# Second-half weights in quarters, own outputs in one bank, U rows by TensorE and integer sums on GpSimd, in the first steps of an mLSTM and feed-forward kernel

## The chip, the cores and the metric

The kernel runs on one core of one Trainium2 chip. The metric is the device time of one execution in microseconds (us). Three runs of the kernel before gave 424.73, 424.93 and 425.49, median 424.93.

## The reference, cut to what matters

Two blocks follow each other. The first is an mLSTM cell over 4 batches, 8 heads, 768 tokens and 40 numbers per head; the second is a multiplicative feed-forward block over the 3072 tokens.

```python
for t in range(S):                                  # per batch and head
    m_new = max(f[t] + m, i[t])
    C = exp(f[t] + m - m_new) * C + exp(i[t] - m_new) * outer(v[t], k[t])
    n = exp(f[t] + m - m_new) * n + exp(i[t] - m_new) * k[t]
    m = m_new
    y[t] = sigmoid(o[t]) * (C @ q[t]) / max(abs(n @ q[t]), 1)
x = y as (3072 tokens, 320)
out = ((x @ w1) * (x @ w2)) @ w3 @ w_out            # w1, w2: 320x1024; w3: 1024x1024; w_out: 1024x320
```

All four weights come as 64-bit floats, so 128 rows of 512 weights are 512 KB.

## The kernel before, in words

The cell is computed in 24 units `n`, each 128 tokens of one batch with all 8 heads; the tokens of a unit are two halves of 64. A unit has a table `pw` (rows of `U`, then `Exp` on ScalarE, then a mask on GpSimd), the scores `ss` (kT by qT), the state update `pc`, the **own output** `ph` (`pw` by `v`, within the halves) and the **output from the state** `pi`. VectorE multiplies `ss` into `pw` (line 402), updates the state (409 or 411, and 419) and makes the output `y` (lines 430 to 457).

The work is written out as steps `s = 0, 1, 2, ...` of the last loop (line 829). In step `s`, TensorE does, in the order of the code: the first part (`up`, 16 passes of 128x256) of the feed-forward products of that step, the transposes of k and q for a later unit (`turn`, where it stands), `up_rest` (the last 64 rows of x, weights `wr`), `ph` and `pi` of unit `s-1`, `ss` and `pc` of unit `s`, then the transposes `px` of a finished `y` (`x_trans`) and those of k and q (`turn`, tile `pt`) of unit `s+1`. `in_order` (line 84) makes the order of the code the order of TensorE; the other engines also run their instructions in the order in which they stand. Step 2 is written out apart, in `between` (line 902): there TensorE does the first `px` and the first `up`. `warm` (line 97) puts matmuls whose result nobody reads into the tile `fill`.

`up` takes two blocks `f` of 128 columns of w1 and w2 at a time: steps 2 and 3 use f = 0..3 (the first halves), step 4 uses f = 4, 5, step 5 uses f = 6, 7, and from step 6 on there are two `up` per step, over all columns.

Weights are fetched as raw 64-bit words (`fetch`, line 216, on the SP queue), scaled on ScalarE (`scale`, lines 196 and 200: the high and the low words), and put together on VectorE (`to_f32`: line 204 shifts, line 205 adds integers; the adder is GpSimd for `w_out` alone). `convert()` does this for the next tile in the list; `n_cvt[s]` says how many times at the end of step `s`. The raw words go into idle parts of later tiles (`idle`, line 529) and, when that list is empty, into four rotating buffers `raw`. The second halves of w1, w2 and `wr` are five tiles (512 columns each), fetched in step 2 between the loads of unit 4 and converted in `between`, at the end of step 2 and in step 3 (`late`). Then come 8 tiles of w_out and 16 of w3, which VectorE also transposes (line 253); step 8 converts three tiles of w3. `fold` (line 258) multiplies finished w3 tiles with w_out (tile `wp`) from step 10 on.

The rows of `U` for a unit are made on VectorE (`rows_of_u`, line 300, up to unit 9); unit 0 takes them by TensorE instead (`spread`, line 277: 16 matmuls of 96 rows by 64 columns into the tile `ub`). `N_DIAG = 2`: for units 0 and 1 `ph` has a PSUM tile of its own and one VectorE addition (line 434); for units 2 to 9 it is laid out in the quarters of `cell[1]` and takes four additions (line 440).

PSUM has 8 banks: two tiles `cell` of two banks each, and four banks that rotate (`mps`) over `px`, `pt`, `pa`, `pb`, `ub`, `ph`, `fill`, `wp`: a new tile waits for the last reader of the tile four allocations earlier.

Of the kernel before, what the change touches and what calls it, by code (L numbers as in the profile page):

```python
# [16 lines left out]
def kernel(  # L17
# [26 lines left out]
    nc = tc.nc  # L44

    B, H, S, D = q.shape
    L = 64
    P = 128
    NT = S // L
    NT2 = S // P  # L50
    NU = NT2 * B
# [39 lines left out]
    def mm(out, lhsT, rhs, start=True, stop=True):  # L91
        in_order(nc.tensor.matmul(out, lhsT=lhsT, rhs=rhs, start=start, stop=stop))  # L92
# [1 line left out]
    def transpose(out, in_, n=P):  # L94
        in_order(nc.tensor.transpose(out, in_, ident[0:n, 0:n]))  # L95

    def warm(n, m=4, small=0):
        bank = mps([P, 4, P], "fill")
        for _ in range(n):
            mm(bank[:, 0:m], ident, ident.unsqueeze(1).to_broadcast([P, m, P]))  # L100
        for i in range(small):
            r = halves[i % 2]
            mm(bank[r, 0, 0:L], ident[r, 0:L], ident[r, 0:L])

    halves = [slice(0, L), slice(L, P)]
    heads = [slice(0, D), slice(DP, DP + D)]
# [2 lines left out]

    NB, NBQ, NBV = 4, 3, 5  # L110
    N_DVE = N_U = 10
    N_DIAG, N_OWN = 2, 10
    q_all = const.tile([P, NBQ * H * DP], FP, name="q_all")
    qbuf = [q_all[:, i * H * DP:(i + 1) * H * DP].rearrange("p (h d) -> p h d", d=DP) for i in range(NBQ)]
    kbuf = [const.tile([P, H, DP], FP, name=f"kbuf{i}") for i in range(NB)]
# [86 lines left out]
    def to_f32(dst, raw, adder):  # L202
        bits = dst.bitcast(U32)
        nc.vector.tensor_scalar(out=bits, in0=raw[:, :, 1], scalar1=3, scalar2=None, op0=OP.logical_shift_left)
        adder.tensor_tensor(out=bits, in0=bits, in1=raw[:, :, 0], op=OP.add)  # L205

    def cols(c0, n):
        return slice(2 * c0, 2 * (c0 + n))
# [7 lines left out]
    def fetch(kind, i, part):  # L216

        if kind == "w12":
            c0 = part * CW
            if i < 2 * KF:  # L220
                wt, src = ((w1, w1_d), (w2, w2_d))[i // KF]
                ko = i % KF
                dst, pieces = wt[:, ko, c0:c0 + CW], [(every, src[ko * 128:(ko + 1) * 128, cols(c0, CW)])]
            else:
                dst, pieces = wr[:, c0:c0 + CW], [(slice(j * REM, (j + 1) * REM), src[KF * P:DM, cols(c0, CW)])
                                                  for j, src in enumerate((w1_d, w2_d))]
        elif kind == "wo":
            dst, pieces = wo[:, i, :], [(every, wo_d.rearrange("(p i) n -> p i n", i=FO)[:, i, :])]
        else:
            dst, pieces = None, [(square, w3_d[i * 128 + part * 64:i * 128 + (part + 1) * 64, cols(j * CQ, CQ)]  # L230
                                  .rearrange("(m r) n -> r m n", m=2)) for j, square in enumerate(squares)]
        pend.append((dst, raw_tile(dst.shape[-1] if dst is not None else CW, pieces), i, part))
# [9 lines left out]
    def convert():  # L242
        if not scaled:
            scale_next()
        dst, raw, ko, half = scaled.pop(0)
        if dst is not None:
            to_f32(dst, raw, nc.gpsimd if dst.shape[-1] == DM else nc.vector)
            return
        w3 = wst.tile([128, CW], FP, name="w3", tag="w3")
        to_f32(w3, raw, nc.vector)  # L250
        if half == 0:
            w3T_t[ko] = wst.tile([128, FO, 128], FP, name="w3T", tag="w3T")
        nc.vector.transpose(out=w3T_t[ko].rearrange("c k (m r) -> c m k r", r=32)[:, 2 * half:2 * half + 2],
                            in_=w3.rearrange("r (m c k) -> r m k c", m=2, k=FO))
        if half:
            turned_w3.append(ko)
# [20 lines left out]
    def spread(n):  # L277


        ub = mps([P, H, L], "ub")  # L280
        for h in range(H):
            r = n % B * H + h
            for x in range(2):
                mm(ub[halves[x], h, :], ident[0:RG, r:r + 1].to_broadcast([RG, L]), U[:, x * L:(x + 1) * L])
        return ub

    def cols_of_u():
# [14 lines left out]

    def weights(n):
        c, b = divmod(n, B)
        src = weights_tile(n) if n else spread(n)
        pw = weights_tile(n)
        for h in range(H):
            nc.scalar.activation(out=pw[:, h, :], in_=src[:, h, :], func=AF.Exp, bias=aT[:, c, b * H + h:b * H + h + 1])  # L308
# [34 lines left out]
    def quarter_work(s, rest, between, late):  # L343
# [10 lines left out]
        if 0 <= n < NU:  # L354
            pw, vt, qT = u_t.pop(n), vbuf[n % NBV], qT_t.pop(n)
            before = before_t.pop(n)
            if n < N_DIAG:
                warm(1)

            if n < N_DIAG:  # L360
                ph = mps([P, H, D1], "ph")
                for hq in range(H):
                    for r in halves:
                        mm(ph[r, hq, :], pw[r, hq, :], vt[r, hq, :])
            for hd in range(H // 2 if n >= N_DIAG else 0):
                for x, e in quarters:
                    hq = hd if x == e else hd + H // 2
                    mm(ph[x][halves[e], hd, :], pw[halves[x], hq, :], vt[halves[x], hq, :])
            for p in range(NP):
                for hip, x in quarters if n >= B else quarters[1:3]:  # L370
                    mm(pi[halves[x], hip, p, :], qT[heads[hip], p, halves[x]], before[x][heads[hip], p, :])
# [154 lines left out]
    load(1)  # L526
    fetch("w12", 2, 0)
    load_o(0)
    idle += [words[:, i * CW:(i + 1) * CW] for words in (w3o_words, wo_words) for i in range(2)]
    fetch("w12", 3, 0)  # L530
    load_o(1)
    fetch("w12", 4, 0)
# [285 lines left out]
    n_seven = [0] * 19 + [1] * 12 + [0]  # L818
    n_down = [0] * 16 + [2] * 5 + [1] * 4 + [0] * 7
    n_out = [0] * 27 + [1, 0, 1, 0, 3]  # L820
    w12 = [("w12", i, part) for part in range(2) for i in range(2 * KF + 1)]
    todo = w12[5:] + [("wo", i, 0) for i in range(FO)] + [("w3", ko, part) for ko in range(FO) for part in range(2)]
    n_cvt = [0, 0, 2, 0, 1, 2, 3, 3, 3] + [2] * 6
    n_fetch = [5, 5, 10]
    pinned, ahead = 32, 9
    behind = ExitStack()
# [2 lines left out]
    for s in range(len(n_up)):  # L829
# [3 lines left out]
            load_u(s + 3)  # L833
        if s < 3:
            if s == 2:
                for _ in range(3):
                    fetch(*todo.pop(0))
            load(s + 2, slice(0, 2))
            if s == 1:
                load_o(2)  # L840
            if s == 2:
                for _ in range(2):
                    fetch(*todo.pop(0))
                fetched = 10
            load(s + 2, slice(2, 3))
            if s:
                load_o(s + 2)
        elif s + 2 < NU:
            load(s + 2)
            load_o(s + 2)  # L850
        if s < NU:
            if s >= B:
                decayed(state[s % B][1], state[s % B][0], s, 0)
# [48 lines left out]
        def between():  # L902
            twice(1)
            weighted(2)
            rows_of_u(3)
            for _ in range(3):
                scale_next()
            for n in range(2):
                x_trans(n)
                if n == 0:  # L910
                    warm(1, small=38)
            for _ in range(3):
                convert()
            turn(2)
            block = up(*now[0])
            weighted(3)
            weights(3)
            masks(3)
            out_gate(2)
            convert()  # L920
            up_rest(*block)

        gated = None
# [4 lines left out]
        with tc.issue_after(gated.ins) if gated else nullcontext():  # L928
            if seven:
                seven[3]()  # L930
            for _ in range({NU: 1, NU + 1: 3}.get(s, 0)):
                next(wsums)
            if s == NU + 1:
                ab_sums(*summed.pop(0))
            if NY <= s - 2 < NU:
                x_turn(s - 2)
            for n in () if s == 1 else (s + 2,) if s < B else (s + 2, s + 3) if s == B else (s + 3,):
                if n < N_U:
                    rows_of_u(n)
            if N_DVE <= s + 1 < NU:  # L940
                shift(s + 1)
                gated = turn(s + 1)
            if s - 2 in range(4 * GT - 1, NU, GT):
                token_sums((s - 2) // GT)
            if s < len(n_up) - 2 and n_out[s + 1] and s > NU + 2:
                ab_sums(*summed.pop(0))
# [6 lines left out]
            cell_psum.close()  # L953
            banks.extend([ps_m] * 3 + [ctx.enter_context(tc.tile_pool(name="ps_x", bufs=4, space=bass.MemoryType.PSUM))] * 4)
        if s in (2, 3):
            turned, converted = 2, converted + (4 if s == 2 else 2)
        while turned < min(s - 1, NY):
            x_trans(turned)
            turned += 1
        if s + 1 < N_DVE and s not in (1, 2):  # L960
            turn(s + 1)
        if s < NU:
            if 0 < s < NU - 1 and s != 2:
                if s != 1:
                    weighted(s + 1)
                if s <= NY:
                    weights(s + 1)
                if 2 < s < N_DVE:
                    twice(s - 1)
                masks(s + 1)  # L970
            if s != 2 and s <= NY:
                out_gate(s)
# [4 lines left out]
            for i, r in enumerate(third):  # L977
                nc.sync.dma_start(out=U_d[i * GC:(i + 1) * GC].rearrange("c r t -> r c t"), in_=U3[r])
        with tc.issue_after(gated.ins) if N_DVE <= s + 1 < NU else nullcontext():
            for _ in range(n_cvt[s] if s < len(n_cvt) else 0):  # L980
                convert()
                converted += 1
        if s >= ahead:
# [40 lines left out]
```

## Time and profile before

| | |
|---|---|
| median of 3 runs | 424.93 us |
| the profiled execution | 425.0 us, span 423.3 us |
| granted TensorE clock | 1.00 |
| PE busy | 414.0 us (98%) |
| PEld busy | 335.9 us (79%) |
| DVE busy | 296.0 us (70%) |
| ACT busy | 183.0 us (43%) |
| POOL busy | 165.4 us (39%) |
| DMA | 46.56 MB, mean 110 GB/s |

PE is TensorE's matmuls, PEld its weight loads, DVE VectorE, ACT ScalarE, POOL GpSimd, SP the queue that issues most transfers. A timeline row has start, duration, engine, line, operation, tile written <- tiles read, shape, count, and in brackets the idle time before it and what ended it. An fp32 matmul appears as two passes, so 16 matmuls are a count of 32. All matmuls have line 92 and all PE transposes line 95 (helpers), so tile names tell them apart.

### The profile page before, as it was taken

The page shows a single profiled execution, that of the slowest core. Times are in us where ns is not written, and L with a number is a line of the kernel's source. Part 1 is how long each engine was busy: PE and PEld are TensorE (multiplying, and loading weights), DVE is VectorE, ACT ScalarE, POOL GpSimd, SP SyncE. Part 2 cuts the span into 40 slices and gives each one's busy share as a digit, 9 for nine tenths or more (in the row PEclk, how much of TensorE's full clock was granted, in tenths as well). Part 3 has the DMA queues.
Part 4 walks back from the last instruction along what each step waited for, and adds up shares of the span by engine and source line. Part 5 has one row for each costly group of instructions (what it writes and reads, how often), then busy time and mean ns, then how long its engine had stood idle before and what let it go on. Part 6 is the DMA issues. An engine that isn't in the chain of part 4 may idle for free.

```text
span 423.3 us, 13077 instructions
## 1 busy us (share of the span) xinstructions
PE 414.0 (98%) x5353; PEld 335.9 (79%) x5353; DVE 296.0 (70%) x561; ACT 183.0 (43%) x516; POOL 165.4 (39%) x219
## 2 busy tenths in 40 slices
PE   8999999999999999999999999999999999999997
PEld 4778788887787787888777778688778779888896
DVE  5676995688948768767635747396877598575972
ACT  3875775567734735843745334253422210210000
POOL 3441373443303303303457343457453487542100
PEclk9999999999999999999999999999999999999999
DMA  8998989689993584863417762733221110000001
GB/s 187 213 152 239 214 153 157 163 180 174 203 192 104 122 175 109 170 104 58 104 35 158 149 139 76 147 73 83 55 54 30 26 39 6 28 2 31 2 33 62
DMA packets 124555, 46.56 MB, mean 110 GB/s; under 512 B 104720, under 2 KB 116304, under 8 KB 124496
## 3 DMA queue, kind: packets, MB, share of 16 engines
q1 hardware_dynamic: 120896, 41.70, 49.2%
q10 hardware_dynamic: 3600, 4.03, 2.7%
q8 instruction: 42, 0.69, 0.7%
q14 instruction: 17, 0.14, 0.1%
HBM read 39.91 MB, written 5.80 MB: 108 GB/s over the span
## 4 chain that ended last, share of the span: by engine, by line
PE 84%; DVE 6%; DMA 3%; issue 2%; SPq 2%; ACT 1%; POOL 1%; DVEq 0%; POOLq 0%; ACTq 0%
PE cell L92 21%; PE pa L92 20%; PE pb L92 13%; PE wp L92 8%; PE o L92 8%; PE po L92 6%; PE p L92 3%; DMA raw<-in_moe_w_dram 2%; PE px L95 2%; PE pt L95 1%; DVE pw L779 1%; DMA q_all<-in_q_dram 1%; SPq L158 1%; DVE ab L693 1%; SPq L139 1%
## 5 line engine op out<-in xcount | busy, mean ns | idle before, releaser
L340 POOL TENSOR_TENSOR state<-state,decay 128x164 f32<-128x164 f32 x40 | 23.2, 581 | 139.7 <-DVE state L409 112.6
L92 PE MATMUL pa<-xT,w 128*128 128x256 f32 x240 | 60.4, 382 | 0.0
L92 PEld LDWEIGHTS pa<-xT,w 128*128 128x128 f32 x240 | 44.4, 190 | 6.4
L308 ACT ACTIVATE pw<-pw,aT 128x64 f32<-128x64 f32 x184 | 46.5, 339 | 0.8 <-DVE pw L300 0.5
L92 PE MATMUL pb<-xT,w 128*128 128x256 f32 x192 | 45.6, 380 | 0.2 <-DVE w L205 0.2
L738 POOL TENSOR_TENSOR ab<-ab,a_sb 128x512 f32<-128x512 f32 x22 | 29.4, 1359 | 31.7 <-DVE ab L693 31.7
L92 PEld LDWEIGHTS pb<-xT,w 128*128 128x128 f32 x192 | 36.4, 190 | 5.5 <-DVE w L205 0.6
L720 POOL TENSOR_TENSOR wo<-wo 128x512 f32<-128x512 f32 x22 | 27.5, 1269 | 29.0 <-DVE wo L695 29.0
L92 PE MATMUL pa<-xT,wr 64*64 64x256 f32 x384 | 37.0, 386 | 0.6 <-DVE wr L205 0.6
L92 PE MATMUL wp<-wo,w3T 128*128 128x320 f32 x128 | 35.9, 433 | 1.4 <-issue 0.8
L92 PE MATMUL pb<-xT,wr 64*64 64x256 f32 x384 | 36.4, 380 | 0.0
L313 POOL TENSOR_SCALAR_AFFINE_SELECT pw<-pw 64x512 f32<-64x512 f32 x48 | 33.2, 692 | 7.9 <-ACT pw L308 6.4
L647 ACT ACTIVATE a_sb<-pa 128x512 f32<-128x512 f32 x24 | 14.3, 597 | 49.9 <-PE pb L92 49.9
L648 DVE TENSOR_TENSOR ab<-pb,a_sb 128x512 f32<-128x512 f32 x24 | 16.4, 688 | 27.4 <-ACT a_sb L647 27.2
L92 PE MATMUL cell<-w3o,ab 128*128 128x320 f32 x128 | 35.5, 433 | 0.0
L92 PEld LDWEIGHTS wp<-wo,w3T 128*128 128x128 f32 x128 | 23.8, 190 | 10.9 <-issue 1.0
L92 PEld LDWEIGHTS cell<-w3o,ab 128*128 128x128 f32 x128 | 24.2, 190 | 9.6 <-ACT wo L711 0.2
L92 PEld LDWEIGHTS pa<-xT,wr 64*64 64x64 f32 x384 | 18.9, 132 | 15.5 <-issue 8.8
L695 DVE SCALAR_TENSOR_TENSOR a_sb<-pa,wo 128x512 f32<-128x512 f32 x12 | 8.3, 689 | 31.1 <-PE pa L92 31.1
L437 ACT COPY h<-cell 64x164 f32<-64x164 f32 x56 | 16.3, 290 | 31.5 <-DVE y L430 31.0
L92 PE MATMUL po<-w3o,ab 128*128 128x320 f32 x96 | 26.4, 433 | 0.0
L92 PEld LDWEIGHTS po<-w3o,ab 128*128 128x128 f32 x96 | 18.1, 190 | 7.3
(185 smaller groups left out, 883.0 us busy)
## 6 DMA issues: line engine op xcount, KB each, us to landing
raw<-in_moe_w_dram SPq DMA_DIRECT2D x64, 128.0 KB, 3.1
kbuf<-in_k_dram SPq DMA_DIRECT2D x24, 160.0 KB, 4.3
v_all<-in_v_dram SPq DMA_DIRECT2D x24, 160.0 KB, 4.7
o_in<-in_o_gate_dram SPq DMA_DIRECT2D x24, 160.0 KB, 4.8
pw<-U_d SPq DMA_DIRECT2D x28, 128.0 KB, 3.5
raw<-in_moe_w_dram SPq DMA_DIRECT2D x5, 512.0 KB, 6.3
raw<-in_moe_w_out_dram SPq DMA_DIRECT2D x8, 320.0 KB, 4.1
out_dram<-o_sb ACTq DMA_DIRECT2D x14, 160.0 KB, 2.4
```

The costliest lines, as they stand in the source:

```text
L92: in_order(nc.tensor.matmul(out, lhsT=lhsT, rhs=rhs, start=start, stop=stop))
L95: in_order(nc.tensor.transpose(out, in_, ident[0:n, 0:n]))
L139: nc.sync.dma_start(out=dst, in_=rows(src, n))
L308: nc.scalar.activation(out=pw[:, h, :], in_=src[:, h, :], func=AF.Exp, bias=aT[:, c, b * H + h:b * H + h + 1])
L313: nc.gpsimd.affine_select(out=pw[r], in_=pw[r], compare_op=OP.is_ge, fill=0.0, base=0, pattern=[[0, H], [1, L]], channel_multiplier=-1)
L340: nc.gpsimd.tensor_tensor(out=new, in0=old, op=OP.mult, in1=decay[:, b * NP:(b + 1) * NP, 2 * c + x:2 * c + x + 1] .to_broadcast([P, NP, D1]))
L437: nc.scalar.copy(out=h[halves[x], 0:H // 2] if x == e else h[halves[x], H // 2:H], in_=ph[x][halves[e]])
L647: nc.scalar.mul(out=a_sb, in_=pa, mul=UP ** -2)
L648: nc.vector.tensor_tensor(out=ab_t[gr][j][:, fs[0]:fs[-1] + 1, t0:t0 + a_sb.shape[-1]], in0=pb, in1=a_sb, op=OP.mult)
L695: nc.vector.scalar_tensor_tensor(out=out, in0=p, scalar=UP ** -2, in1=q, op0=OP.mult, op1=OP.add)
L720: aside_by.tensor_tensor(out=kept[j][:, 1:4:2], in0=kept[j][:, 1:3], in1=kept[j][:, 3:4].to_broadcast([128, 2, TH]), op=OP.add)
L738: aside_by.tensor_tensor(out=t[:, f:FO:FH, :], in0=t[:, f:FO:FH, :], in1=a, op=OP.mult)
```

## The change

Four things change in the first ten steps; the rest of the program is the same.

1. The second halves of w1, w2 and `wr` become two quarters (256 columns): ten tiles for five. The first five go into idle words of `wo` and are fetched in step 2 ahead of the loads of unit 4; the other five go into words of `w3o` and are fetched in step 3. `load_o` moves one step later from unit 3 on. Step 2 fetches 5 tiles of 256 KB in place of 5 of 512 KB.
2. The integer sum (line 205) of these ten tiles is done on GpSimd; the shift stays on VectorE. The five first quarters are converted at the end of step 2 and in step 3, the five last ones in step 4, ahead of `out_gate` and behind the copies of the transposes of unit 5. `n_cvt` becomes 3, 5, 2, 3, 3, 4 for steps 2, 4, 5, 6, 7, 8 (before: 2, 1, 2, 3, 3, 3): step 7 converts three tiles of w_out (before: two, and one of w3), and step 8 four tiles of w3 (before three).
3. `N_DIAG = 6`: the own outputs of units 2 to 5 also get a bank of their own and one addition.
4. The `U` rows of units 4 and 5 come from `spread` (their `Exp` reads `ub` from PSUM), no longer from `rows_of_u`.

In `between`, `rows_of_u(3)` moves behind three `convert()` (the fourth is dropped there), and `warm(1, small=38)` becomes `warm(2)`.

```diff
-    N_DIAG, N_OWN = 2, 10
+    N_DIAG, N_OWN, SPREAD = 6, 10, (0, 4, 5)
...
         if kind == "w12":
-            c0 = part * CW
+            c0, n = ((0, CW), (CW, CW // 2), (CW + CW // 2, CW // 2))[part]
...
-            to_f32(dst, raw, nc.gpsimd if dst.shape[-1] == DM else nc.vector)
+            to_f32(dst, raw, nc.vector if dst.shape[-1] == CW else nc.gpsimd)
...
-                mm(ub[halves[x], h, :], ident[0:RG, r:r + 1].to_broadcast([RG, L]), U[:, x * L:(x + 1) * L])
+                t0 = n // B * P + x * L
+                mm(ub[halves[x], h, :], ident[0:RG, r:r + 1].to_broadcast([RG, L]), U[:, t0:t0 + L])
...
-        src = weights_tile(n) if n else spread(n)
+        src = spread(n) if n in SPREAD else weights_tile(n)
...
-            if n < N_DIAG:
+            if n < 2:
                 warm(1)
...
-    idle += [words[:, i * CW:(i + 1) * CW] for words in (w3o_words, wo_words) for i in range(2)]
+    idle += [w3o_words[:, i * CW:(i + 1) * CW] for i in range(2)]
+    idle += [words[:, i * CW // 2:(i + 1) * CW // 2] for words, order in ((wo_words, range(5)), (w3o_words, (4, 0, 1, 2, 3)))
+             for i in order]
...
-    w12 = [("w12", i, part) for part in range(2) for i in range(2 * KF + 1)]
+    w12 = [("w12", i, part) for part in range(3) for i in range(2 * KF + 1)]
...
-    n_cvt = [0, 0, 2, 0, 1, 2, 3, 3, 3] + [2] * 6
+    n_cvt = [0, 0, 3, 0, 5, 2, 3, 3, 4] + [2] * 6
...
             if s == 2:
-                for _ in range(3):
+                for _ in range(5):
                     fetch(*todo.pop(0))
             load(s + 2, slice(0, 2))
             if s == 1:
                 load_o(2)
             if s == 2:
-                for _ in range(2):
-                    fetch(*todo.pop(0))
+                load_o(3)
                 fetched = 10
             load(s + 2, slice(2, 3))
-            if s:
-                load_o(s + 2)
         elif s + 2 < NU:
-            load(s + 2)
-            load_o(s + 2)
+            load(s + 2, slice(0, 2))
+            if s == 3:
+                for _ in range(5):
+                    fetch(*todo.pop(0))
+                fetched = 15
+            load(s + 2, slice(2, 3))
+            load_o(s + 1)
...
-            rows_of_u(3)
             for _ in range(3):
                 scale_next()
             for n in range(2):
                 x_trans(n)
                 if n == 0:
-                    warm(1, small=38)
+                    warm(2)
             for _ in range(3):
                 convert()
+            rows_of_u(3)
             turn(2)
...
             out_gate(2)
-            convert()
             up_rest(*block)
...
-                if n < N_U:
+                if n < N_U and n not in SPREAD and s != B:
                     rows_of_u(n)
...
         if s + 1 < N_DVE and s not in (1, 2):
             turn(s + 1)
+        if s == B:
+            for _ in range(n_cvt[s]):
+                convert()
+                converted += 1
+            for n in (6, 7):
+                rows_of_u(n)
```

More of the change, by code (lines that the diff above doesn't have):

```diff
@@ L95, in transpose, with warm @@
         in_order(nc.tensor.transpose(out, in_, ident[0:n, 0:n]))
-    def warm(n, m=4, small=0):
+    def warm(n, m=4):
         bank = mps([P, 4, P], "fill")
@@ L100, in warm @@
             mm(bank[:, 0:m], ident, ident.unsqueeze(1).to_broadcast([P, m, P]))
-        for i in range(small):
-            r = halves[i % 2]
-            mm(bank[r, 0, 0:L], ident[r, 0:L], ident[r, 0:L])
     halves = [slice(0, L), slice(L, P)]
@@ L222, in fetch @@
                 ko = i % KF
-                dst, pieces = wt[:, ko, c0:c0 + CW], [(every, src[ko * 128:(ko + 1) * 128, cols(c0, CW)])]
+                dst, pieces = wt[:, ko, c0:c0 + n], [(every, src[ko * 128:(ko + 1) * 128, cols(c0, n)])]
             else:
-                dst, pieces = wr[:, c0:c0 + CW], [(slice(j * REM, (j + 1) * REM), src[KF * P:DM, cols(c0, CW)])
+                dst, pieces = wr[:, c0:c0 + n], [(slice(j * REM, (j + 1) * REM), src[KF * P:DM, cols(c0, n)])
                                                   for j, src in enumerate((w1_d, w2_d))]
@@ L841 @@
             if s == 2:
-                for _ in range(2):
-                    fetch(*todo.pop(0))
+                load_o(3)
                 fetched = 10
             load(s + 2, slice(2, 3))
-            if s:
-                load_o(s + 2)
         elif s + 2 < NU:
-            load(s + 2)
-            load_o(s + 2)
+            load(s + 2, slice(0, 2))
[5 more added lines that the diff above has]
+            load_o(s + 1)
+        elif s + 2 == NU:
+            load_o(s + 1)
         if s < NU:
@@ L955 @@
         if s in (2, 3):
-            turned, converted = 2, converted + (4 if s == 2 else 2)
+            turned, converted = 2, converted + (3 if s == 2 else 2)
         while turned < min(s - 1, NY):
@@ L979 @@
         with tc.issue_after(gated.ins) if N_DVE <= s + 1 < NU else nullcontext():
-            for _ in range(n_cvt[s] if s < len(n_cvt) else 0):
+            for _ in range(n_cvt[s] if s < len(n_cvt) and s != B else 0):
                 convert()
```

## The prediction

> **What bounds the kernel now.** I read the page first: TensorE is busy nearly throughout, and the chain that ended last runs over it.
>
> ```profile
> PE 414.0 (98%) x5353; PEld 335.9 (79%) x5353; DVE 296.0 (70%) x561; ACT 183.0 (43%) x516; POOL 165.4 (39%) x219
> PE 84%; DVE 6%; DMA 3%; issue 2%; SPq 2%; ACT 1%; POOL 1%; DVEq 0%; POOLq 0%; ACTq 0%
> ```
>
> So only time that TensorE idles, or spends on passes of no use, can be won, and every useful pass that is added costs its full time, unless it falls into a wait. The windows by stage tell where it idles: 58 to 104 us has none at all, the changed stretch a little.
>
> ```profile
> 28.00:50.00 22.00, 20.90 (x407) 17.45 (x406) 15.32 (x33) 15.32 (x38) 5.47 (x9) 1.00 0.95 199
> 50.00:58.00 8.00, 8.00 (x177) 7.01 (x176) 7.49 (x20) 5.29 (x16) 4.95 (x9) 1.00 1.03 246
> 58.00:104.00 46.00, 46.00 (x751) 39.38 (x753) 35.02 (x72) 29.87 (x78) 21.21 (x33) 1.00 0.85 162
> 104.00:106.50 2.50, 1.87 (x77) 1.51 (x70) 2.47 (x5) 2.26 (x8) 0.00 (x0) 1.00 0.86 234
> ```
>
> Columns: stretch, length, then busy us (instructions) of PE, PEld, DVE, ACT, POOL; clock, DMA share, GB/s. Last, the timeline of the changed steps and of step 9: what TensorE waits for, and the rows that price the additions.
>
> ```profile
> 9.07 1.98 PE L92 MATMUL ub<-gates,ident 96*64 96x64 f32 x32
> 20.93 1.07 PE L92 MATMUL ph<-v_all,pw 64*64 64x41 f32 x30
> 21.78 0.25 PE L92 MATMUL cell<-state,qT 40*64 40x41 f32 x1
> 23.76 3.39 PE L92 MATMUL fill<-ident 128*128 128x512 f32 x78
> 25.29 0.24 POOL L486 COPY y<-y 128x64 f32<-128x64 f32 x1 [1.75 <-DVE y L457]
> 40.56 0.56 PEld L92 LDWEIGHTS cell<-qT,kT 40*64 40x64 f32 x32 [0.47 <-ACT qT L330]
> 44.94 1.16 PEld L92 LDWEIGHTS pb<-xT,w 128*128 128x128 f32 x6 [0.59 <-DVE w L205]
> 47.05 0.13 PEld L92 LDWEIGHTS pa<-xT,wr 64*64 64x64 f32 x1 [0.95 <-DVE wr L205]
> 57.78 0.89 POOL L205 TENSOR_TENSOR wo<-wo,raw 128x320 uint32<-128x320 uint32 x1
> 102.99 0.39 DVE L204 TENSOR_SCALAR w<-raw 128x512 uint32<-128x512 uint32 x1
> 103.52 0.69 DVE L205 CUSTOM_DVE_ANT_0 w<-raw,w 128x1024 uint16<-128x1024 uint16 x1
> 104.24 1.12 DVE L253 STREAM_TRANSPOSE w3T<-w 128x512 f32<-128x512 f32 x1
> 105.29 1.25 DVE L648 TENSOR_TENSOR ab<-pb,a_sb 128x512 f32<-128x512 f32 x2
> 105.99 8.88 PE L92 MATMUL wp<-wo,w3T 128*128 128x320 f32 x32 [0.63 <-DVE ab L648]
> ```
>
> The waits before the change are for qT (its copy stands on ScalarE behind the scaling of raw words) and for the converted second halves, w at 44.94 and `wr` at 47.05. At step 9 VectorE is the late one: three w3 conversions run without a gap into `ab`, and `wp` wants the bank that `ab` frees.
>
> **Step 2 to the px of step 5 (27.08 to 49.78 before).** Start to start, the groups take: px 0.38, pt pair 0.87, up 3.46 (two of 1.73 in the chain), up_rest 0.91 (54.59 to 55.50), ph, pi, ss, pc 1.82 (55.50 to 57.32). Step 2 without ph and pi is 6.54, steps 3 and 4 without px 7.06 each: 20.66 of work in 22.70, so 2.04 us of waiting.
> Won: the px of unit 1 starts at 27.08, behind 76 small passes, though its input was ready at 25.53 (POOL row). Two fills (4 passes of 0.43) end at 25.5, so px starts at 25.57: -1.5. The waiting for w and `wr` goes, since the first quarters are half the words, shifted in step 3, and five GpSimd sums of about 0.71 finish by about 43.5, ahead of pa and pb (about 43.4 and 45.1). The 0.71 is an estimate: a sum of 128x320 takes 0.89, one of 128x164 (line 340) 0.47, 256 columns lie between. The qT wait goes too, since three scalings of 256 columns fit ahead of the copies. Together -2.04.
> Paid: `ub` of unit 4 stands between pt and pa of step 4. Its price is from the same group at 9.07, 1.91 to what follows; bounds are 1.98 above and 0.85 below, the `ph` group, whose 32 passes run two side by side. I take 1.91, the same operation. [...]
> `ph` in a bank of its own runs on two quadrants, 0.85 (20.93 to 21.78) for 0.44 in `cell`: +0.41 each, for units 2 and 3 +0.82.
> A new wait: in step 3 the bank of `ph` is that of `pa`, four allocations back, so `ph` waits for `a_sb` (line 647), which starts 0.29 after up_rest and takes 0.60: +0.91, between 0 (if banks turn otherwise) and 0.91. In steps 4 and 5 the bank is that of a pt, long free; in step 6 that of the first of two `up`, read while the second rests: 0. Behind this wait stand pi, ss, pc and all of step 4.
> Sum: -1.5 -2.04 +1.91 +0.82 +0.91 = +0.1; px of step 5 at 49.9.
>
> **Step 5.** Before, it had no wait. Now it needs the last quarters, whose five scalings stand on ScalarE behind the qT copy of unit 5 (about 51.4; a pair each 0.69, by the 0.395 spacing of 320 columns and 0.555 of 512) and whose shifts stand on VectorE behind y of unit 3. That y ended 2.84 after the reciprocal at 51.94; now the additions are one of 0.50 for four of 1.34, the reciprocal comes at about 50.3 and y ends at 53.1. First shift 53.4, first sum 54.1, second 54.8, third 55.5, fourth 56.2, `wr` 56.9. TensorE is through pt at 51.1 and `ub` of unit 5 at 53.0; pa waits until 54.15, its second matmul until 54.85, then all is there: waiting 1.4. With `ub` 1.91 and `ph` 0.41 the step is 3.7 longer. If `ub` were shorter, the wait would grow by as much. Sums of 0.47 or 0.95 (bounds: the 164 columns and a little over the 320) make it 0.5 less or 0.6 more.
> What speaks against this move is in the rows: shifts of 320 columns took 0.66 beside a GpSimd mask (55.93), 512 columns without one 0.39. [...]
> VectorE's relief elsewhere (five sums of 0.69, four times 0.84 for the additions, two `rows_of_u` of 0.70) I cost at nothing: no TensorE wait from 50 to 104 hangs on it. The moved loads (o gates a step later, v and o behind the quarters on SP) I also cost at nothing: ScalarE has work ahead of each o gate, and steps 4 and 5 start no earlier than before.
>
> **Steps 6 and 9.** `ph` of unit 5: +0.41. Step 8 converts four w3 tiles for three. VectorE is gapless there, one tile is 2.29 (102.99 to 105.29), and `ab` stands behind it: `wp` starts 2.29 later. Step 7 is lighter by one, but has its slack in a wait of 0.25 for `a_sb`, and y of step 8 follows TensorE, not VectorE's queue. +2.29, between 0 and 2.9 (the first tile, beside GpSimd, took that).
>
> **Sum** against the profiled 425.0 (0.07 over the median, as good as equal): +0.1 +3.7 +0.4 +2.3 = +6.5, so 431.5. Low end: `ub` 0.9 in step 4 (-1.0), no wait for `a_sb` (-0.9), short sums (-0.5), and half of the 2.3 hidden, 428.0. High end: long sums (+0.6) and half or more of the late transfers below, 434.
>
> **Rivals.**
> Hidden conversion: VectorE makes up the fourth w3 tile and step 9 keeps its 0.63 wait. For it: step 8 comes after a lighter step 7. Against: no gap from 97.9 to 106.5. 431.5 - 2.3 = 429.2. Chance 0.13.
> Late quarters: the third quarter's scaling stands ahead of the kT and qT copies of unit 3 on ScalarE. The three 512 KB tiles were scaled at 33.81, 36.50 and 38.30, each after waiting for its transfer. Quarters at half their spacing are there by 35.2; from about 36.0 on the wait reaches TensorE, and if the third came at 38.3 as before, it would cost 2.3: 433.8. Chance 0.12.
> Faster: steps 2 to 6 are paced by the supply of weights, and the added passes run beside their neighbours, as the 32 `cell` passes of `ph` do in 0.44. Then 3.5 is won there and two groups of 0.43 are paid, the sums being ready: 422.3. It decides as soon as all added TensorE time, 5.5 in my rows, and the new waits stay under 3.5. For it: two of the three waits before are for weights. Against: the row at 9.07, and 50 to 104 us without a TensorE wait. Chance 0.07, and 0.02 that it ends within 0.2%.
> That the order is not what the text says is ruled out by the list of instructions: two `ub` groups ahead of pa, ten GpSimd sums, four w3 tiles in step 8.
>
> **How the numbers follow.** My forecast has 0.66, the rivals 0.13, 0.12 and 0.09. Two tenths of a per cent, 0.85 us, is about what a measurement of this kernel can tell from no change. Slower: 0.66 + 0.13 + 0.12 = 0.91; same 0.02; faster 0.07. The range 428.0 to 434.0 takes in the first three cases and the bounds of `ub`, the sums and the new wait.
>
> **What would show it.** Right: two `ub` groups near 41 to 53 us of about 1.9; `ph` of unit 2 waiting for `a_sb`; px of step 5 near 49.9; pa of step 5 waiting for a GpSimd sum of line 202 and starting near 54; px of step 6 near 61 (before 57.3); `wp` waiting about 2.9 for `ab`. Wrong: px of step 6 at or before 58, `ub` under 1 us, or `wp` with a wait of 0.6.

## The result and the profile after

The changed kernel takes 430.19 us (430.0 to 431.0), the kernel before, run beside it, 424.86 us: ratio 1.0126, 95% interval 1.0109 to 1.0144. The profiled execution took 430.02 us, span 428.3 us. Taken again later it was 430.81 against 425.34, ratio 1.0129 (1.0093 to 1.0165). Ratios leave out the runs in a slow state, such as those over 1.5% above the fastest of the same kernel; medians include them.

First the page of the changed kernel, engines and chain of waits, then its windows by stage (stretch, length, busy us of PE, PEld, DVE, ACT, POOL, clock, DMA share, GB/s).

```profile
PE 417.0 (97%) x5343; PEld 338.6 (79%) x5343; DVE 287.8 (67%) x547; ACT 183.3 (43%) x526; POOL 172.3 (40%) x229
PE 88%; DVE 5%; DMA 2%; issue 2%; POOL 1%; ACT 1%; SPq 0%; DVEq 0%; POOLq 0%
```

```profile
28.00:50.00 22.00, 21.50 (x462) 18.37 (x460) 11.79 (x30) 14.09 (x41) 10.39 (x16) 1.00 1.00 196
50.00:62.00 12.00, 8.97 (x160) 7.04 (x160) 5.07 (x11) 4.94 (x18) 7.45 (x11) 0.86 0.92 189
62.00:108.00 46.00, 46.00 (x655) 39.56 (x653) 26.80 (x59) 28.74 (x77) 20.89 (x32) 0.96 0.57 127
108.00:113.00 5.00, 5.00 (x169) 4.03 (x168) 4.52 (x8) 3.85 (x10) 0.00 (x0) 1.00 0.87 225
```

The loss is in the second row: TensorE, without a gap there before, idles 3.0 of 12 us, and the granted clock is 0.86. The stretch of steps 2 to 4 (first row) is better filled than before, and that of step 9 (last row) has lost its gap. Where the clock fell is seen by cutting the trace at the starts of its 3.41 us stretches:

```profile
48.94:52.35 3.41, 1.76 (x24) 1.20 (x21) 2.39 (x7) 3.41 (x12) 2.31 (x4) 1.00 0.92 128
52.35:55.76 3.41, 3.41 (x9) 2.71 (x9) 1.56 (x3) 2.00 (x10) 3.35 (x7) 0.50 0.92 304
59.18:62.59 3.41, 1.54 (x71) 1.37 (x64) 1.58 (x5) 0.00 (x0) 0.00 (x0) 1.00 0.47 62
62.59:66.00 3.41, 3.41 (x14) 3.04 (x13) 2.70 (x7) 2.72 (x8) 1.57 (x3) 0.50 0.02 5
```

Two stretches in which TensorE idled 1.65 and 1.87 us are each followed by one at half clock. The timeline has the two idle times, and the rows that the prediction priced:

```profile
8.24 1.15 PE L92 MATMUL ub<-gates,ident 96*64 96x64 f32 x32
39.08 1.15 PE L92 MATMUL ub<-gates,ident 96*64 96x64 f32 x32
40.16 0.70 PE L92 MATMUL pa<-xT,w 128*128 128x256 f32 x2
50.29 3.00 POOL L202 TENSOR_TENSOR w<-w,w3o 128x256 uint32<-128x256 uint32 x4 [1.10 <-DMA q_all<-in_q_dram]
51.10 3.23 PE L92 MATMUL pa<-xT,w 128*128 128x256 f32 x8 [1.60 <-POOL w L202]
54.12 2.70 PE L92 MATMUL pb<-xT,w 128*128 128x256 f32 x8
61.88 0.27 PE L92 MATMUL cell<-vw,kbuf 64*40 64x41 f32 x3 [1.87 <-issue]
112.17 8.78 PE L92 MATMUL wp<-wo,w3T 128*128 128x320 f32 x32
```

`pa` of step 5 waits 1.60 us for its GpSimd sum, as forecast. The second gap, inside `pc` of the same step, is ended by "issue": nothing that the profile shows. `wp` of step 9 waits for nothing.

### The profile page after: what moved, and what is told of

Same layout as the page of the kernel before. It is cut to its first block, busy times and chain, and to the rows that moved or that the text cites. A ratio compares the mean times of both kernels' runs of the same rounds, so it can differ in the third digit from the quotient of the medians.

```text
span 428.3 us, 13081 instructions
## 1 busy us (share of the span) xinstructions
PE 417.0 (97%) x5343; PEld 338.6 (79%) x5343; DVE 287.8 (67%) x547; ACT 183.3 (43%) x526; POOL 172.3 (40%) x229
## 4 chain that ended last, share of the span: by engine, by line
PE 88%; DVE 5%; DMA 2%; issue 2%; POOL 1%; ACT 1%; SPq 0%; DVEq 0%; POOLq 0%
PE pa L92 22%; PE cell L92 21%; PE pb L92 14%; PE wp L92 8%; PE o L92 8%; PE po L92 6%; PE p L92 3%; PE pt L95 2%; PE px L95 2%; DMA kbuf<-in_k_dram 1%; DVE pw L779 1%; DMA q_all<-in_q_dram 1%; PE fill L92 1%; PE ph L92 1%; DVE ab L693 1%
## 5 line engine op out<-in xcount | busy, mean ns | idle before, releaser
L92 PE MATMUL pa<-xT,w 128*128 128x256 f32 x240 | 62.7, 393 | 1.6 <-POOL w L202 1.6
L92 PEld LDWEIGHTS pa<-xT,w 128*128 128x128 f32 x240 | 45.6, 195 | 9.0 <-POOL w L202 2.2
L306 ACT ACTIVATE pw<-pw,aT 128x64 f32<-128x64 f32 x168 | 42.4, 336 | 2.5 <-DVE pw L298 2.2
L311 POOL TENSOR_SCALAR_AFFINE_SELECT pw<-pw 64x512 f32<-64x512 f32 x48 | 33.6, 699 | 10.1 <-ACT pw L306 8.6
```

The lines of the kernel that those rows point to most:

```text
L311: nc.gpsimd.affine_select(out=pw[r], in_=pw[r], compare_op=OP.is_ge, fill=0.0, base=0, pattern=[[0, H], [1, L]], channel_multiplier=-1)
```

## Experiments

One fact is needed to read them. Single executions of the kernel before and of most versions spread by 4 us or more, those of the changed kernel by 2.4: `px` of unit 0 starts between 21.0 and 25.9 us in 14 profiles, by where the full clock sets in (4.6 to 11.2 us) and whether a gap falls into step 1. So medians and profiles are both given, and traces are compared by the starts of `px`, step by step, between executions that began alike.

**The kernel before, once more.** No edit.

> The kernel before once more, unchanged. In its first profile the granted TensorE clock was recorded from 10.98 us on and the U rows of unit 0 (tile ub) took 1.98 us; in the changed kernel it was recorded from 4.56 us on and the same group took 1.15, though nothing had changed up to there. Theory A (the clock's rise falls at another moment in each execution): this run shows another moment, or at least times of the start that differ between executions, and 424.7 to 425.5 us in all. Theory B (the changed program itself starts earlier): the clock again rises near 11 us and the ub group again takes about 1.98. It also shows whether the 0.79 us gap at 141.7 us that no wait explains comes back.

Measured: 425.31 us against 425.63, ratio 1.0013 (0.9984 to 1.0042); single times 424.24 to 428.36. This is the spread to judge the rest by. Theory A held: the full clock is recorded from 6.23 us on, and the `ub` group takes 1.15 us. Over all 14 profiles the same group takes 1.15 us in the ten whose record begins at 4.6 to 6.8 us, 1.75 where it begins at 10.49, and 1.98 in the three from 10.98 on. The gap at 141.7 us came back too, 1.00 us long.

**Conversions out of step 5's way** (on the changed kernel; the texts on record call this version early_sums):

```diff
-    n_cvt = [0, 0, 3, 0, 5, 2, 3, 3, 4] + [2] * 6
+    n_cvt = [0, 0, 3, 3, 2, 2, 3, 3, 4] + [2] * 6
```

> The changed kernel with the conversions of the five last quarters begun a step sooner: three at the end of step 3 (behind the output gate of unit 3), two in step 4, in place of five in step 4. No work is added or left out. Theory A (step 5 is late because the sums of the last quarters are late, and the wait of 1.6 us ahead of pa also halves the granted clock in the windows after it): pa of step 5 starts right behind ub, the clock stays at 1.00, step 5 takes about 9.5 us in place of 15.1, the time falls by 4 to 6 us to 424 to 426. Rival B (the slow passes of step 5 come from something else, such as transfers or the stall of 1.9 us in the middle of pc): only the wait of 1.6 goes, 428.5. Rival C (the early scalings hold up a_sb of step 4 on ScalarE, and the wait moves there): 429 to 431.

Measured: 424.58 us, ratio 0.9977 (0.9946 to 1.0008). So nearly the whole loss hangs on the place of three conversions. The profiled execution happened to be the longest of ten (428.58 us), with a gap of 1.37 us in step 1 and a half-clock stretch behind it (clock 0.76 from 21 to 28 us).

**The same kernel once more** (early_again in the texts), for a profile of a usual run:

> The kernel early_sums once more (three quarter conversions in step 3 and two in step 4, in place of none and five). Theory 'wait': the loss of the change hangs on the 1.60 us wait of pa for its GpSimd sum in step 5, since behind that wait the granted clock goes to half for 3.4 us; without it 424 to 425 us, clock 1.00 or a single half-clock stretch, px of step 5 to px of step 6 about 9.5 us. Rival 'sum of terms' (the prediction's): only 1.4 us of 430.2 go, 428.8 us.

Measured: 424.93 us, ratio 0.9991 (0.9962 to 1.002), profiled span 422.7 us, clock 1.00. From `px` of step 5 to that of step 6 it takes 9.69 us.

**The changed kernel once more:**

> The changed kernel unchanged, for the spread of its time and a second profile. Theory 'wait': pa of step 5 waits 1.60 us for its GpSimd sum in every execution, the granted clock falls to half behind it in most, and the 1.9 us gap inside pc of the same step comes and goes in length: 428 to 431 us, median near 430. Rival 'accident': the loss was a property of those four executions, and the median is below 427 us, with a profile that shows neither half-clock stretch nor wait.

Measured: 430.81 us (429.11 to 431.46), all six runs with a clock of 0.991 to 0.996. Its profile began like that of the run above (full clock from 6.51 and 6.59 us), so the two can be laid side by side. First this kernel, then the one with early conversions:

```profile
52.51 2.31 PE L92 MATMUL pa<-xT,w 128*128 128x256 f32 x8 [1.60 <-POOL w L202]
63.28 0.27 PE L92 MATMUL cell<-vw,kbuf 64*40 64x41 f32 x3 [3.54 <-issue]
```

```profile
50.90 0.92 PE L92 MATMUL pa<-xT,w 128*128 128x256 f32 x3
57.96 0.27 PE L92 MATMUL cell<-vw,kbuf 64*40 64x41 f32 x4 [0.16 <-issue]
```

| `px` starts (us) | before, again | early conversions, again | changed, again |
|---|---|---|---|
| unit 1 | 25.55 | 24.34 | 24.61 |
| step 5 | 48.44 | 48.47 | 48.41 |
| step 6 | 56.34 | 58.16 | 63.48 |
| step 7 | 68.20 | 70.61 | 77.61 |
| step 9 | 103.83 | 106.19 | 113.19 |
| step 10 | 124.32 | 125.78 | 132.78 |
| step 12 | 156.06 | 156.37 | 163.37 |
| end | 422.49 | 422.71 | 429.71 |

The two right columns agree to 0.06 us at step 5 and are 7.00 us apart from step 7 to the end: 1.60 of wait, 3.4 more of the "issue" gap, 0.3 of further waiting in `pa` and `pb`, and 1.7 in step 6. The windows from 64 to 78 us show that last part, first the changed kernel, then early conversions:

```profile
64.00:78.00 14.00, 14.00 (x205) 11.66 (x204) 5.72 (x13) 6.68 (x18) 5.22 (x8) 0.88 0.50 96
```

```profile
64.00:78.00 14.00, 14.00 (x212) 11.94 (x211) 6.73 (x16) 7.42 (x21) 6.83 (x10) 1.00 0.52 97
```

In the first profile of the changed kernel the same 5.4 us of step 5 came in another split: wait 1.60, half clock in `pa` and `pb` about 1.8, gap 1.87.

**A fill in the wait** (on the changed kernel): TensorE works through the wait on a fill.

```diff
+        if s == 5:
+            warm(2)
```

> The changed kernel with two fills (four passes of 0.43 us into a tile that nobody reads) ahead of the first up of step 5, where TensorE waits 1.6 us for the sums. The sums are as late as before. Theory A (the idle stretch itself halves the clock for 3.4 us windows): without idle time the clock stays at 1.00, pa and pb take 1.73 each where they took about 3.0 and 2.5, and the whole is 2 to 4 us faster, 426 to 428, though TensorE does more. Rival B (the clock falls for another reason, or the passes are slow because of the sums): 430 to 430.5, no better, with the same slow passes.

Measured: 431.07 us, ratio 1.014 (1.0108 to 1.0173). In the profile step 5 keeps the full clock, has no gap, and takes 11.29 us against 15.08 on record. But this execution had a 1.24 us gap in step 1 and 10.24 us of half clock from 20.73. All four runs have a clock of 0.988 to 0.992, and three of them have no profile. So the half clock is absent when the wait is filled, in the one execution that can be seen. What is slow there stands ahead of step 5, whose `px` starts at 53.52 us; from there to the end it takes 375.84 us, against 381.30 in both profiles of the changed kernel and 374.24 in that of early conversions. That the other three runs lost their time in the same way is not shown.

**What "issue" is: moving the instructions** (on the changed kernel), with the small passes of before:

```diff
-                    warm(2)
+                    warm(1, small=38)
```

> The changed kernel with the one fill and 38 small passes of before in place of two fills; everything else as after. Theory 'block': the 1.87 us gap of TensorE inside pc (60.0 to 61.9 us, ended by nothing that the profile shows) comes from TensorE's instructions, which arrive in 16 KB packets of 256: it lies at instruction 1985 = 193 + 7 x 256 in the list, and 68 more instructions ahead of it move the border to another place, where 256 instructions take longer than a packet. Then no gap in pc of step 5; px of unit 1 about 1.0 us later, the gap and the half-clock stretch behind it gone (-1.9, -1.7): about 427.6 us. Rival 'place': the gap belongs to pc in that step (state update, GpSimd or VectorE) and stays: about 431 us. In both the 1.6 us wait of pa stays, and a half-clock stretch behind it.

Measured: 428.84 us (427.7 to 429.56), ratio 1.0073 (1.0053 to 1.0094). The text on record counts 68 more instructions; they are 148 (each fp32 matmul is two passes and two weight loads: the 16 of the `ub` group are 32 of each in the trace). There is no gap in `pc` of step 5, and the time is 1.35 us under the median on record although `px` of unit 1 starts 1.6 us later against that of unit 0. The `pa` wait stayed, and a gap appeared elsewhere:

```profile
52.90 0.48 PE L92 MATMUL pa<-xT,w 128*128 128x256 f32 x1 [1.59 <-POOL w L205]
110.88 0.23 PE L92 MATMUL cell<-vw,kbuf 64*40 64x41 f32 x2 [1.05 <-issue]
```

The first instruction after each such gap can be counted in the list of TensorE's instructions (from 0; its matmuls, weight loads and the sequencer's few), and compared with the packets of the queue that the page calls "instruction":

```profile
q8 instruction: 42, 0.69, 0.7%
```

42 packets of 16 KB, for 10,799 instructions: one for 256. The numbers of the gaps:

| kernel | instruction | gap | packet ended | gap ended |
|---|---|---|---|---|
| changed | 1985 = 193 + 7 x 256 | 1.87 | 60.42 | 61.88 |
| changed, again | 1985 | 3.54 | 61.82 | 63.28 |
| early conversions | 1985 | 1.06 | 60.45 | 62.12 |
| early conversions, again | 1985 | 0.16 | 56.66 | 57.96 |
| before | 4545 = 193 + 17 x 256 | 0.79 | 140.97 | 142.47 |

In the 14 profiles every "issue" gap of TensorE of 0.39 us or more behind the first 30 instructions, 23 of them, lies at an instruction of 193 + k x 256, and ends 1.3 to 1.7 us after that block's packet. No block began less than 1.29 us after its packet among the first dozen of any profile.

**Moving the borders on purpose** (on early conversions):

```diff
-    warm(1, 2)
+    warm(0, small=13)
...
-    warm(1, 2)
+    warm(0, small=13)
```

> early_sums with 13 small passes in place of each of two 256-column fills in the first 10 us: the same TensorE time within 0.2 us, but 96 more instructions ahead of everything that follows, so that the borders of the 256-instruction packets lie elsewhere (349 and 1889 in the old count instead of 449 and 1985). Theory 'block': no gap before the scores of step 1 (1.2 to 1.4 us in four profiles) or in pc of step 5; by the spacing of early_again the shortest block before 60 us is then 3.8 us long instead of 2.9. Fewer half-clock stretches, median 423.5 to 424.5 us against 424.6 to 424.9 for the same kernel without it. [...]

Measured: 427.87 us, ratio 1.0054 (1.0023 to 1.0085): worse by 3 us than without. The rule on places held, the expected time did not. The gaps left instructions 449 and 1985 and came at 705, 1729 and 2497, again 193 + k x 256, which now fall into other groups:

```profile
22.23 0.76 PE L92 MATMUL ph<-v_all,pw 64*64 64x41 f32 x11 [1.62 <-issue]
54.81 0.79 PE L92 MATMUL ub<-gates,ident 96*64 96x64 f32 x18 [1.06 <-issue]
75.62 0.23 PE L92 MATMUL cell<-vw,kbuf 64*40 64x41 f32 x1 [0.73 <-issue]
```

I had picked the shift by the time that TensorE takes for each 256 instructions. What decides as much is when the packet starts: 2.9 us behind the first instruction of the block before it at the first of these gaps, 2.1 at the second, 0.95 at the third. That delay cannot be read off a list of instructions.

**The fourth w3 conversion alone** (on the kernel before):

```diff
-    n_cvt = [0, 0, 2, 0, 1, 2, 3, 3, 3] + [2] * 6
+    n_cvt = [0, 0, 2, 0, 1, 2, 3, 2, 4] + [2] * 6
```

> The kernel before with n_cvt of steps 7 and 8 as 2 and 4 (before: 3 and 3), the fourth w3 conversion of the change alone. The prediction's term: VectorE is 2.29 us later with ab, wp waits 2.9 us, and the time is 2.3 us longer (427.5 us). Rival 'bank': wp waits for ab only because its PSUM bank was read by it; the allocator gives wp another bank here (that of the second pa, freed by the ScalarE copy), so wp waits for nothing and the time is that of before or 0.6 us less.

Measured: 424.13 us, ratio 0.9967 (0.994 to 0.9994): the one version here that beats the kernel before, by 1.2 us in the medians. VectorE is late with `ab`, as forecast, and `wp` does not care:

```profile
103.79 1.13 DVE L253 STREAM_TRANSPOSE w3T<-w 128x512 f32<-128x512 f32 x1
106.09 1.11 DVE L253 STREAM_TRANSPOSE w3T<-w 128x512 f32<-128x512 f32 x1
107.12 1.25 DVE L648 TENSOR_TENSOR ab<-pb,a_sb 128x512 f32<-128x512 f32 x2
```

```profile
104.70 1.51 PE L92 MATMUL wp<-wo,w3T 128*128 128x320 f32 x5
```

`wp` starts 0.39 after `px`, 2.4 us before `ab`. The program's list of banks says why: its bank is the one of the second `pa`, which ScalarE's copy frees, and no longer that of the first `pb`, which VectorE frees with `ab`.

**Sums on VectorE** (on the changed kernel):

```diff
-            to_f32(dst, raw, nc.vector if dst.shape[-1] == CW else nc.gpsimd)
+            to_f32(dst, raw, nc.gpsimd if dst.shape[-1] == DM else nc.vector)
```

> The changed kernel with the integer sums of the ten quarters on VectorE again (they take 0.75 us each on GpSimd; 256 columns on VectorE an estimated 0.35, half of the 0.69 of 512). If the wait in step 5 is set by the sums on GpSimd, it gets shorter by 0.4 to 0.8 us and the half-clock stretch behind it may go: 427 to 429 us. Rival: the wait is set by the scalings on ScalarE and the shift behind them (the first sum starts 0.35 us after the first shift can), so it stays at 1.2 to 1.6 us, or grows because y stands ahead on VectorE: about 430 us.

Measured: 429.81 us, ratio 1.0102 (1.0066 to 1.0137). The wait stays, though a sum takes 0.42 us there instead of 0.75:

```profile
54.65 0.76 DVE L455 SCALAR_TENSOR_TENSOR y<-o_in,h 128x320 f32<-128x320 f32 x1
55.33 0.28 DVE L201 TENSOR_SCALAR w<-w3o 128x256 uint32<-128x256 uint32 x1
55.75 0.42 DVE L202 CUSTOM_DVE_ANT_0 w<-w3o,w 128x512 uint16<-128x512 uint16 x1
```

```profile
56.23 2.33 PE L92 MATMUL pa<-xT,w 128*128 128x256 f32 x8 [1.55 <-DVE w L202]
```

The shift starts as `y` ends and the sum follows, so the wait is set by a chain: `y`, shift, sum. The sum got 0.33 shorter, but `y` takes 0.76 for the 0.48 in the first profile of the changed kernel. GpSimd, without the sums ahead of it, runs `vw` (54.33 to 55.06) beside `y` here; there it stood idle while `y` ran. With a `y` of 0.48 the wait would be about 1.3 us (an estimate), so what stands ahead of the sum sets most of it. No half-clock stretch follows the wait in this profile.

**Two parts undone** (both on early conversions). Own outputs back in `cell`:

```diff
-    N_DIAG, N_OWN, SPREAD = 6, 10, (0, 4, 5)
+    N_DIAG, N_OWN, SPREAD = 2, 10, (0, 4, 5)
```

> early_sums with N_DIAG = 2: the own outputs of units 2 to 5 back in cell, four additions on VectorE for each. By the prediction's term (0.41 us of TensorE each) it gains 1.6 us on early_sums: about 423.0 us, ph 0.44 us long. Rival: the four additions (1.34 us for 0.50) make y, and with it px, late in steps 2 to 6, and nothing is gained or up to 1 us is lost: 424.6 to 425.6 us, with waits of px for y.

Measured: 427.11 us, ratio 1.0021 (0.999 to 1.0051), single times 422.98 to 431.61; the profiled execution had a 3.66 us gap at instruction 1985 and four half-clock stretches. The group itself is 0.63 us long in `cell` against 1.02 in its own bank, 0.39 less, about as the term said; the median cannot show it.

U rows of units 4 and 5 back on VectorE:

```diff
-    N_DIAG, N_OWN, SPREAD = 6, 10, (0, 4, 5)
+    N_DIAG, N_OWN, SPREAD = 6, 10, (0,)
```

> early_sums with SPREAD = (0,): the U rows of units 4 and 5 by VectorE again, no ub groups in steps 4 and 5. By the prediction's term, 1.91 us each, it gains 3.8 us on early_sums, 420.8 us; by the rows of the trace after, 1.08 us each (39.08 to 40.16), 2.2 us, 422.4 us. Rival: two rows_of_u of 0.70 us and the additions behind them make a wait elsewhere (pa for its sum or px for y), and less than 1 us is gained: 423.6 us or more.

Measured: 425.71 us, ratio 1.0014 (0.999 to 1.0039). The two groups are gone, and in step 5 waits take their place. The profile also has "issue" gaps of 1.29 and 0.78 us at instructions 4801 and 6081, so the median does not price the two groups alone:

```profile
50.58 1.97 PE L92 MATMUL pa<-xT,w 128*128 128x256 f32 x8 [0.37 <-DVE h L432]
54.16 1.56 PE L92 MATMUL pb<-xT,w 128*128 128x256 f32 x6 [1.18 <-POOL w L202]
```

**The fills alone** (on the kernel before): `rows_of_u(3)` behind the conversions, and

```diff
-                    warm(1, small=38)
+                    warm(2)
```

> The kernel before with one part of the change alone: in step 2 two fills in place of one and 76 small passes, and the U rows of unit 3 behind the three conversions. From the rows: the px of unit 1 starts 1.5 us sooner. Theory A (these 1.5 us reach the end): 423.4. Rival B (the waits of steps 3 and 4 for w, wr and the qT copy are set by transfers and conversions, and take it back): 424.9, with longer waits there.

Measured: 426.12 us, ratio 0.9997 (0.9974 to 1.0019). `px` of unit 1 comes 2.70 us after that of unit 0 instead of 4.31. By step 5 it is more than lost again (25.29 us from there to `px` of step 5, before 22.70): TensorE arrives earlier at weights that are not ready, with waits of 0.8 for qT, 0.9 for w and 0.6 for `wr`.

## Why the prediction was right, and where only its sum was

The direction and the size came out: 430.19 against 431.5, with pa of step 5 waiting for a GpSimd sum of line 202. The steps tell another story.

- **Fills, -1.5: right.** The interval from `px` of unit 0 to that of unit 1 went from 4.31 to 2.70 us, -1.6; undone alone in the changed kernel it came back to 4.30.
- **Steps 2 to 4, +1.6 behind that `px`: too much.** From `px` of unit 1 to that of step 5 the changed kernel takes 0.6 us longer (22.70 to 23.28), and 0.9 in the later pair of executions (22.89 to 23.80). The `ub` group and the `a_sb` wait below were charged 1.7 too much; so only about 1.0 to 1.3 of the 2.04 us of waiting was won. From `px` of unit 0 to step 5 the forecast was +0.1; measured are -1.0 (27.01 to 25.98) and -0.7 (27.20 to 26.50).
- **`ub`, 1.91 each: mis-sized; 1.08** (39.08 to 40.16). The row that priced it, at 9.07 us, ran ahead of the full clock: in that execution the record of full clock begins at 10.98, in the changed one at 4.56, and the same group of unit 0 took 1.98 there and 1.15 here. The clock column counts the time ahead of the record as full (1.00 for 7.60 to 10.90 us), so the row looked sound. The lower bound, the 0.85 of `ph` at 20.93, was much nearer: that row ran behind the start of the record. In all three groups the passes start two by two, 6 to 7 ns apart: a pair every 107 ns in the row at 9.07, every 58 ns in `ph` at 20.93 and in `ub` at 39.08 of the changed kernel. What differs is the pace, ahead of the record of full clock and behind it, not the pairing.
- **`ph` waiting for `a_sb`, +0.91: wrong.** It started at 35.78, ahead of the copy at 36.01. Like the wait at step 9, it came from assuming that a bank is always the one of four allocations back. The program's list of banks shows them out of turn: this `ph` has the bank of the first `pt` of its step, `wp` of step 9 that of the second `pa`.
- **`ph` in its own bank, +0.41: right** (0.39 in the group).
- **Sums on GpSimd, 0.71: right**, 0.75 (x4 in 3.00), not the upper bound of 0.95. But the shifts were longer beside the sums: the three for step 5 that begin at 50.80 us or later, each while a sum runs, take 0.40, 0.51 and 0.60 us, against 0.25 to 0.29 for the other seven quarters, and each ends 0.15 us after that sum.
- **Wait in step 5, 1.4: right in mechanism**, 1.60 and some 0.3 behind it. TensorE came there earlier than forecast, by the shorter `ub`, and so did `y` and the sums; the two offset each other.
- **What is behind the wait, 0 in the sum: missed.** In the first profile the stretches with the gaps of 1.60 and 1.87 us were each followed by 3.41 us at half clock, up to 1.7 us of loss each; in the second only the one with the larger gap was. And step 5 holds a border of an instruction block, 1.9 to 3.5 us. Between the two executions that began alike they are 5.1 of the 7.0 us (3.4 and 1.7).
- **Step 9, +2.29: wrong, -0.9.** Step 9 takes 19.59 us instead of 20.49. The fourth conversion costs nothing, and the change of bank removes the wait of 0.63.

So without the wait of 1.4 the forecast would still have been 5.1 us slower than before, and the kernel measured without it is as fast as before. The terms overcharged (`ub`, the `a_sb` wait, step 9) and the missing one (clock and gap) cancelled. The figure was good by that luck; the forecast that something in step 5 would be late was good by its reasons.

The rivals: the hidden conversion was right on step 9, and lower than the truth only because the step-5 costs were missing from it. Late quarters did not happen: pa of step 4 had no wait. "Faster" had the right bound, the supply of weights. With the conversions early all that it won is paid back by `ub`, `ph` and a fuller step 5, and early conversions ends level.

## What to carry to other kernels

Before pricing an operation by a row, see at which clock that row ran, above all in the first 11 us (`ub` here: 1.98 against 1.15 us). A wait on an engine that is otherwise full can cost more than its length (here 1.60 us of wait in a step that took 5.4 us longer): look at what the clock does behind it, and try to move the late work one step earlier before anything else. Read banks and queues out of the built program rather than by a rule; a wait seen in the trace may vanish when an allocation moves.

## What the runs showed of the hardware

- **The clock.** In the first profile of the changed kernel it changes between full and half in stretches of 3.41 us (47.79 us of full clock, 14 of them, then 3.41 of half, 6.83 of full, 3.41 of half). Partly idle stretches stood ahead of the half clock: 1.65 of 3.41 us idle was followed by it in one execution of the changed kernel and not in the other, where 2.15 us was; a gap of 1.24 us in step 1 was followed by it in the kernel with the fill in the wait (10.24 us of half clock) and not in the one with the fills alone (1.00 from 15 to 28 us). The share of idle time alone does not decide; what else does is open.
- **Instructions.** TensorE's come in packets of 256 (42 packets for 10,799), and among the first dozen of each of the 14 profiles no block starts less than 1.29 us after its packet. Groups of small passes use up 256 in under 3 us (57.26 to 60.01 in the changed kernel, ahead of the gap of 1.87), so TensorE can run dry: 0.4 to 3.7 us in these profiles. Why a packet starts late is not settled. In both profiles of the changed kernel that of block 1985 starts 11.8 us after `px` of step 5, in both of early conversions 7.1 to 7.2 us after, although the clock and the waits differ. The changed kernel issues four w_out transfers of 320 KB in that step, early conversions two. But early conversions with the own outputs in `cell` issues two as well, and there the packet starts 10.1 us after and the gap is 3.66 us; and in the changed kernel the four had landed 0.5 to 1.3 us before the packet started. So their number alone does not decide it, and the cause stays open.
